# Linear attention and a multiplicative FFN on one core: q, k and v with 64 partitions of nine tokens per head, the heads split over the two partition halves, and the first batch in two head groups

## The chip, the core and the metric

The kernel runs on one core of one Trainium2 chip. The kernel's tiles in the on-chip memory (SBUF) have up to 128 partitions, their first axis; its matmuls leave their results in tiles in PSUM. The metric is device time in microseconds (us), lower is better. Each version was executed several times; the text gives the median and, in brackets, the lowest and highest.

## The reference, cut to what matters

Eight batches of eight heads, 576 tokens of 64 features each, go through linear attention; the result, 4608 tokens of 512 features, goes through two products, an elementwise product and two more products.

```python
def phi(x):  return np.where(x > 0, x, np.exp(x) - 1.0) + 1.0
# q, k, v: (8, 8, 576, 64) float32
kv  = einsum('bhsd,bhse->bhde', phi(k), v);  z = sum(phi(k), axis=2)
num = einsum('bhsd,bhde->bhse', phi(q), kv)
den = einsum('bhsd,bhd->bhs',  phi(q), z)[..., None] + 1e-06
x   = (num / den) transposed to (4608, 512)
a, b = x @ w1, x @ w2                      # 512 x 1024 each
out = (a * b @ w3) @ w_out                 # 1024 x 1024, 1024 x 512
```

phi is computed as max(x + 1, min(exp(x), 1)): one exp on ScalarE, one min and one add-max on VectorE. The kernel multiplies w3 by w_out once ("wf"), so that each token needs w1, w2 and wf only.

Of the kernel before, what the change touches and what calls it, by code (L numbers as in the profile page):

```python
# [8 lines left out]
F32 = mybir.dt.float32  # L9
# [9 lines left out]
def kernel(  # L19
# [18 lines left out]
    NJ = 4  # L38
    R = S - NJ * P
    JW = H * NJ * D  # L40
    RW = (H // 2) * D
    n_chunks = NTOK // NCH

# [3 lines left out]
    for b in range(0, B, 2):  # L47
        for key in [("J", b, j) for j in range(NJ)] + [("J", b + 1, j) for j in range(NJ)] + [("R", b, 0)]:
            tile_of[key] = len(order)
            order.append(key)  # L50
        tile_of["R", b + 1, 0] = tile_of["R", b, 0]
# [32 lines left out]
    vt = wpool.tile([P, NJ, H, D + 1], BF16)  # L84
    vr = wpool.tile([P, H // 2, D + 1], BF16)
    nc.gpsimd.memset(vt[:, :, :, D:D + 1], 1.0)
    nc.gpsimd.memset(vr[:, :, D:D + 1], 1.0)
# [4 lines left out]
    def load_qkv(name, src, b):  # L92
        t = ld.tile([P, JW + RW], F32, tag="ld", name=f"{name}32")
        ins = nc.sync.dma_start(
            out=t[:, 0:JW].rearrange("p (h x) -> p h x", h=H),
            in_=src[b, :, 0:NJ * P, :].rearrange("h (p j) d -> p h (j d)", j=NJ),
        )
        for hh in range(2):
            nc.sync.dma_start(
                out=t[hh * R:(hh + 1) * R, JW:].rearrange("p (h d) -> p h d", d=D),  # L100
                in_=src[b, hh * 4:(hh + 1) * 4, NJ * P:S, :].rearrange("h p d -> p h d"),
            )
        raw[name, b] = t
        return ins


    def phi_steps(name, b, dst_j, dst_r):
        x = raw[name, b]
        e = e_p.tile([P, JW + RW], BF16, tag="e", name="e")
        xv = x[:, 0:JW].rearrange("p (h j d) -> p h j d", h=H, j=NJ)  # L110
        ev = e[:, 0:JW].rearrange("p (h j d) -> p h j d", h=H, j=NJ)

        def ex(j0):
            nc.scalar.activation(  # L114
                out=ev[:, :, j0:j0 + 2, :], in_=xv[:, :, j0:j0 + 2, :], func=AF.Exp)
            nc.vector.tensor_scalar_min(  # L116
                out=ev[:, :, j0:j0 + 2, :], in0=ev[:, :, j0:j0 + 2, :], scalar1=1.0)

        def exr():
            nc.scalar.activation(out=e[:, JW:], in_=x[:, JW:], func=AF.Exp)  # L120
            nc.vector.tensor_scalar_min(out=e[:, JW:], in0=e[:, JW:], scalar1=1.0)

        def st(j):
            nc.vector.scalar_tensor_tensor(  # L124
                out=dst_j[:, j, :].rearrange("p (h d) -> p h d", h=H),
                in0=xv[:, :, j, :], scalar=1.0, in1=ev[:, :, j, :], op0=ALU.add, op1=ALU.max)

        def sr():
            nc.vector.scalar_tensor_tensor(
                out=dst_r, in0=x[:, JW:], scalar=1.0, in1=e[:, JW:],  # L130
                op0=ALU.add, op1=ALU.max)

        return dict(e0=lambda: ex(0), e2=lambda: ex(2), eR=exr, s0=lambda: st(0),
                    s1=lambda: st(1), s2=lambda: st(2), s3=lambda: st(3), sR=sr)

    ph = {}

    def k_steps(b):
        kj = phi_p.tile([P, NJ, DM], BF16, tag="kj", name="kj")
        kr = phi_p.tile([P, RW], BF16, tag="kr", name="kr")  # L140
        ph["k", b] = (kj, kr)
        return phi_steps("k", b, kj, kr)

    def q_steps(b):
        qj = phi_p.tile([P, NJ, DM], BF16, tag="qj", name="qj")
        qr = phi_p.tile([P, RW], BF16, tag="qr", name="qr")
        ph["q", b] = (qj, qr)
        return phi_steps("q", b, qj, qr)

    def v_unit(b, parts=(0, 2, 4)):  # L150
        x = raw["v", b]
        for j0 in parts:
            copy = nc.vector.tensor_copy if b == 0 and j0 else nc.scalar.copy
            if j0 < NJ:
                copy(out=vt[:, j0:j0 + 2, :, 0:D],  # L155
                     in_=x[:, 0:JW].rearrange("p (h j d) -> p j h d", h=H, j=NJ)[:, j0:j0 + 2])
            else:
                copy(out=vr[:, :, 0:D], in_=x[:, JW:].rearrange("p (h d) -> p h d", d=D))
# [3 lines left out]

    def kv_unit(b):

        kj, kr = ph["k", b]
        kvp = at_ps.tile([P, 2, 512], F32, tag="at", name="kvp")
        for hp in range(KC):
            o = kvp[:, hp // 2, (hp % 2) * 130:(hp % 2) * 130 + 130]
            for j in range(NJ):
                nc.tensor.matmul(  # L170
                    o, kj[:, j, hp * P:(hp + 1) * P],
                    vt[:, j, 2 * hp:2 * hp + 2, :].rearrange("p h e -> p (h e)"),
                    start=(j == 0), stop=False)
            hh, i = divmod(hp, 2)
            rows = slice(hh * R, (hh + 1) * R)
            nc.tensor.matmul(  # L176
                o, kr[rows, i * P:(i + 1) * P],
                vr[rows, 2 * i:2 * i + 2, :].rearrange("p h e -> p (h e)"),
                start=False, stop=True)
        t = att.tile([P, KC, 2, D + 1], BF16, tag="kv", name="kv")  # L180
        kvs[b] = t
        nc.vector.tensor_tensor(  # L182
            out=t.rearrange("p (a i) h e -> p a (i h e)", a=2), in0=kvp[:, :, 0:260],
            in1=mask.rearrange("p (a i) h e -> p a (i h e)", a=2), op=ALU.mult)
        return kvp


    def qt_load(b, part):
        qj, qr = ph["q", b]
        if part == 0:  # L190
            t = att.tile([P, NJ, KC, P], BF16, tag="qt", name="qt")
            src = qj.rearrange("p j c -> p (j c)")
            dst = t.rearrange("p j c t -> p (j c) t")
        else:
            t = att.tile([P, 2, P], BF16, tag="qtr", name="qtr")
            src, dst = qr, t
        qts[b, part] = t
        nc.sync.dma_start(out=dst, in_=src, transpose=True)

    def nat_unit(b, j):  # L200
# [4 lines left out]
        if j == 0:  # L205
            xns[b] = att.tile([P, NJ, H, D], BF16, tag="xn", name="xn")
        if j < NJ:
            n, dst = P, xns[b][:, j]
        else:
            n = R  # L210
            dst = xns[b, "R"] = att.tile([R, H, D], BF16, tag="xnr", name="xnr")
        for hp in range(KC):
            if j < NJ:
                w = qts[b, 0][:, j, hp, :]
            else:
                hh, i = divmod(hp, 2)
                w = qts[b, 1][:, i, hh * R:(hh + 1) * R]
            nc.tensor.matmul(nd[0:n, hp // 2, (hp % 2) * 130:(hp % 2) * 130 + 130], w,  # L218
                             t[:, hp].rearrange("p h e -> p (h e)"), start=True, stop=True)
        v4 = nd[0:n, :, 0:260].rearrange("p a (x e) -> p a x e", e=D + 1)  # L220
# [7 lines left out]
    def xt_load(b, part):  # L228
        if part == 0:
            i = tile_of["J", b, 0]  # L230
            dst = xt[:, i:i + NJ].rearrange("p j c t -> p (j c) t")
            src = xns[b].rearrange("p j h e -> p (j h e)")
        else:
            dst = xt[:, tile_of["R", b, 0], :, (b % 2) * R:(b % 2 + 1) * R]
            src = xns[b, "R"].rearrange("p h e -> p (h e)")
        nc.sync.dma_start(out=dst, in_=src, transpose=True)


    def first_tr():
        qj, _ = ph["q", 0]  # L240
        qt = qts[0, 0] = att.tile([P, NJ, KC, P], BF16, tag="qt", name="qt")
        tp = at_ps.tile([P, 2, 8, P], BF16, tag="at", name="tp")
        for j in range(NJ):
            for hp in range(KC):
                nc.tensor.transpose(  # L245
                    tp[:, j // 2, (j % 2) * KC + hp, :], qj[:, j, hp * P:(hp + 1) * P], ident)
            if j % 2:
                nc.vector.tensor_copy(
                    out=qt[:, j - 1:j + 1].rearrange("p j c t -> p (j c) t"), in_=tp[:, j // 2])

    def first_kv():
        kvp = kv_unit(0)
        t = kvz["z"] = att.tile([P, KC, 2, D], BF16, tag="kvz", name="kvz", bufs=1)
        n = kvz["n"] = att.tile([P, KC, 2, D], BF16, tag="kvn", name="kvn", bufs=1)
        m4 = mask.rearrange("p (a i) h e -> p a (i h) e", a=2)
        v4 = kvp[:, :, 0:260].rearrange("p a (x e) -> p a x e", e=D + 1)
        for dst, src in ((t, v4[:, :, :, D:D + 1].to_broadcast([P, 2, 4, D])),
                         (n, v4[:, :, :, 0:D])):
            nc.vector.tensor_tensor(
# [264 lines left out]
```

## The kernel before: the parts that the change touches

576 tokens are four times 128 and 64 left over. So each of q, k and v of a batch came as one large DMA over all 128 partitions (four tokens per partition and head, 1 KB rows) and two small ones for the rest, which put four heads on each partition half.

```python
NJ = 4; R = S - NJ * P          # R = 64 tokens left over
def load_qkv(name, src, b):
    t = ld.tile([P, JW + RW], F32, tag="ld", name=f"{name}32")
    ins = nc.sync.dma_start(                                   # 128 partitions, 1 KB rows
        out=t[:, 0:JW].rearrange("p (h x) -> p h x", h=H),
        in_=src[b, :, 0:NJ * P, :].rearrange("h (p j) d -> p h (j d)", j=NJ))
    for hh in range(2):                                        # the rest, 256 B rows
        nc.sync.dma_start(
            out=t[hh * R:(hh + 1) * R, JW:].rearrange("p (h d) -> p h d", d=D),
            in_=src[b, hh * 4:(hh + 1) * 4, NJ * P:S, :].rearrange("h p d -> p h d"))
```

A kv unit forms phi(k)ᵀ·[v, 1] of a batch, for each pair of heads four matmuls of 128 rows and one of 64. An nd unit multiplies transposed phi(q) with it (numerator and denominator), divides, and a transposing DMA brings the quotient to the layout xt that the FFN needs.

```python
def kv_unit(b):
    for hp in range(KC):                      # 4 pairs of heads
        for j in range(NJ):
            nc.tensor.matmul(o, kj[:, j, hp * P:(hp + 1) * P], vt[:, j, 2*hp:2*hp+2, :], ...)
        nc.tensor.matmul(o, kr[rows, ...], vr[rows, ...], start=False, stop=True)   # 64 rows
    # one multiplication by a mask, PSUM to SBUF
...
def o_unit(c, m):                             # 8 matmuls, then the output tile of 128 tokens
    if kind == "J": nc.gpsimd.dma_start(out=dst[:, j, :], in_=o_sb)
    else:           # two DMAs of 64 rows
```

The first batch goes step by step through whole tensors (phi of k, phi of q, 16 transposes, v, kv, nd), then FFN chunk 0 (512 tokens) follows. Loads of later batches are issued by the SP engine far ahead, into five buffers; weights and outputs are issued by GpSimd (POOL). From chunk 1 on a fixed schedule places the pieces of attention between FFN units ("F", 8 matmuls) and output units ("O").

## Time and profile before

| | before |
|---|---|
| time, first three runs | 285.53 us (283.41 to 285.62) |
| span of the profiled run, granted TensorE clock | 281.9 us, 0.975 |
| busy share of PE (TensorE), DVE (VectorE), ACT (ScalarE) | 86%, 55%, 47% |
| DMA: data moved, DMA queue of q, k, v (share of the 16 engines' span) | 51.63 MB, 55.3% |

The page of a profile cuts the span into 40 slices and gives busy tenths for each; "PEclk" is the clock that TensorE was granted, in tenths.

### The profile page before, as it was taken

How to read it: one execution, taken by the hardware profiler on the slowest of the kernel's cores; microseconds unless marked ns; L12 is line 12 of the kernel's file. 1: busy time of each engine (PE TensorE's matmuls, PEld its weight loads, DVE VectorE, ACT ScalarE, POOL GpSimd, SP SyncE). 2: the span in 40 equal slices, each digit the busy share in tenths (PEclk: the TensorE clock that was granted, in tenths of full speed). 3: DMA queues.
4: the chain of work that ended last, by engine and by line, in shares of the span. 5: the costliest groups of instructions: out<-in, count | busy, mean ns of one | idle time of the engine just before them, and what ended most of it. 6: DMA issues, size and time to landing. Idle time of an engine off the chain costs nothing.

```text
span 281.9 us, 3730 instructions
## 1 busy us (share of the span) xinstructions
PE 241.8 (86%) x1301; PEld 116.7 (41%) x1320; DVE 155.6 (55%) x326; ACT 132.7 (47%) x203; POOL 35.6 (13%) x70
## 2 busy tenths in 40 slices
PE   0045899999559977999999999999999999999990
PEld 0032245555225433545544444554544444444430
DVE  0863268418725995984895697499447221222300
ACT  2612467894804555455456555545532333333330
POOL 2380021000100000010110011011001001101021
PEclk9999999999959988999999999999999999999997
DMA  7999999999999979999999898906502501202122
GB/s 197 303 193 201 262 260 265 172 301 232 268 215 309 278 154 242 240 260 262 241 251 274 181 326 201 235 37 154 127 23 67 143 2 74 74 2 76 74 92 58
DMA packets 81139, 51.63 MB, mean 183 GB/s; under 512 B 48096, under 2 KB 77792, under 8 KB 81120
## 3 DMA queue, kind: packets, MB, share of 16 engines
q1 hardware_dynamic: 71744, 36.71, 55.3%
q0 software_dynamic: 9376, 14.68, 21.9%
q8 instruction: 10, 0.16, 0.2%
q14 instruction: 9, 0.07, 0.1%
HBM read 38.80 MB, written 9.44 MB: 171 GB/s over the span
## 4 chain that ended last, share of the span: by engine, by line
PE 76%; DMA 11%; DVE 6%; ACT 2%; issue 2%; SPq 1%; POOL 0%; POOLq 0%; DVEq 0%; ACTq 0%
PE a_ps L285 22%; PE b_ps L285 20%; PE o_ps L304 19%; DMA q<-in_q_dram 6%; PE wf_ps L356 4%; PE kvp L170 4%; DMA xt<-xn 3%; PE nd L218 3%; DMA qt<-qj 2%; PE kvp L176 2%; DVE qj L124 1%; PE w3p L350 1%; PE nd L269 1%; DVE xn L224 1%; ACT vt L155 1%
## 5 line engine op out<-in xcount | busy, mean ns | idle before, releaser
L285 PEld LDWEIGHTS <-w_sb 128*128 128x128 bf16 x576 | 55.8, 100 | 76.2 <-issue 10.1
L291 DVE TENSOR_TENSOR ab<-a_sb,b_ps 128x512 bf16<-128x512 f32 x72 | 49.2, 685 | 67.5 <-PE b_ps L285 57.4
L285 PE MATMUL a_ps<-xt,w_sb 128*128 128x512 bf16 x288 | 77.7, 390 | 8.8 <-DMA xt<-xn 6.1
L285 PE MATMUL b_ps<-xt,w_sb 128*128 128x512 bf16 x288 | 77.5, 389 | 0.0
L290 ACT COPY a_sb<-a_ps 128x512 f32<-128x512 f32 x72 | 41.7, 587 | 60.6 <-PE a_ps L285 59.3
L304 PE MATMUL o_ps<-wf_sb,ab 128*128 128x512 bf16 x272 | 66.2, 379 | 0.9 <-issue 0.2
L307 ACT COPY o_sb<-o_ps 128x512 f32<-128x512 f32 x36 | 21.1, 586 | 54.8 <-PE o_ps L304 52.8
L311 POOL DMA_DIRECT2D out_dram<-o_sb x32 | 17.4, 545 | 191.6 <-ACT o_sb L307 191.6
L304 PEld LDWEIGHTS <-ab 128*128 128x128 bf16 x288 | 27.6, 98 | 31.0
L124 DVE SCALAR_TENSOR_TENSOR qj<-q,e 128x512 bf16<-128x512 f32 x32 | 20.8, 684 | 0.4
L124 DVE SCALAR_TENSOR_TENSOR kj<-k,e 128x512 bf16<-128x512 f32 x32 | 20.6, 685 | 0.2
L224 DVE TENSOR_TENSOR xn<-nd,r 128x512 bf16<-128x512 f32 x28 | 19.4, 691 | 1.0
L116 DVE TENSOR_SCALAR e<-e 128x1024 bf16<-128x1024 bf16 x32 | 13.5, 422 | 10.5 <-ACT e L114 10.5
L114 ACT ACTIVATE e<-k 128x1024 bf16<-128x1024 f32 x16 | 16.9, 1060 | 4.7 <-DMA k<-in_k_dram 4.7
L114 ACT ACTIVATE e<-q 128x1024 bf16<-128x1024 f32 x16 | 16.4, 1058 | 2.1 <-DMA q<-in_q_dram 2.1
L170 PE MATMUL kvp<-vt,kj 128*128 128x130 bf16 x128 | 13.9, 233 | 3.3 <-ACT vt L155 1.7
L155 ACT CAST vt<-v 128x1024 bf16<-128x1024 f32 x15 | 15.0, 1045 | 1.7 <-DMA v<-in_v_dram 1.7
L245 PE MATMUL tp<-ident,qj 128*128 128x128 bf16 x16 | 2.2, 306 | 15.7 <-DVE qj L124 13.4
L356 PE MATMUL wf_ps<-wo_sb,w3t 128*128 128x512 bf16 x61 | 14.8, 379 | 0.3 <-issue 0.2
L182 DVE TENSOR_TENSOR kv<-kvp,mask 128x520 bf16<-128x520 f32 x8 | 5.6, 699 | 15.8 <-PE kvp L176 15.8
L218 PE MATMUL nd<-kv,qt 128*128 128x130 bf16 x112 | 11.0, 221 | 1.4 <-DMA qt<-qj 1.4
L218 PEld LDWEIGHTS <-qt 128*128 128x128 bf16 x112 | 8.6, 98 | 8.0 <-DMA qt<-qj 1.9
(49 smaller groups left out, 130.2 us busy)
## 6 DMA issues: line engine op xcount, KB each, us to landing
k<-in_k_dram SPq DMA_DIRECT2D x8, 1024.0 KB, 8.0
q<-in_q_dram SPq DMA_DIRECT2D x8, 1024.0 KB, 9.0
v<-in_v_dram SPq DMA_DIRECT2D x8, 1024.0 KB, 7.6
out_dram<-o_sb POOLq DMA_DIRECT2D x32, 256.0 KB, 4.1
w_sb<-in_moe_w_dram POOLq DMA_DIRECT2D x8, 256.0 KB, 7.1
w3b<-in_moe_w_dram POOLq DMA_DIRECT2D x8, 256.0 KB, 8.5
k<-in_k_dram SPq DMA_DIRECT2D x16, 64.0 KB, 7.1
q<-in_q_dram SPq DMA_DIRECT2D x16, 64.0 KB, 7.5
```

The source lines that it names most:

```text
L114: nc.scalar.activation(out=ev[:, :, j0:j0 + 2, :], in_=xv[:, :, j0:j0 + 2, :], func=AF.Exp)
L124: nc.vector.scalar_tensor_tensor(out=dst_j[:, j, :].rearrange("p (h d) -> p h d", h=H), in0=xv[:, :, j, :], scalar=1.0, in1=ev[:, :, j, :] ...
L155: copy(out=vt[:, j0:j0 + 2, :, 0:D], in_=x[:, 0:JW].rearrange("p (h j d) -> p j h d", h=H, j=NJ)[:, j0:j0 + 2])
L170: nc.tensor.matmul(o, kj[:, j, hp * P:(hp + 1) * P], vt[:, j, 2 * hp:2 * hp + 2, :].rearrange("p h e -> p (h e)"), start=(j == 0), stop=False)
L218: nc.tensor.matmul(nd[0:n, hp // 2, (hp % 2) * 130:(hp % 2) * 130 + 130], w, t[:, hp].rearrange("p h e -> p (h e)"), start=True, stop=True)
L224: nc.vector.tensor_tensor(out=dst.rearrange("p (a x) e -> p a x e", a=2), in0=v4[:, :, :, 0:D], in1=r[0:n].unsqueeze(3).to_broadcast([n, 2 ...
L285: nc.tensor.matmul(ps, w[:, kc, f * P:(f + 1) * P], xt[:, 4 * c:4 * c + 4, kc, :], start=(kc == 0), stop=(kc == KC - 1))
L290: nc.scalar.copy(out=a_sb, in_=a_ps)
L291: nc.vector.tensor_mul(out=abs_[c][:, f, :], in0=a_sb, in1=b_ps)
L304: nc.tensor.matmul(o_ps, ab[:, f, m * P:(m + 1) * P], wf_sb[:, f, :], start=(f == 0), stop=(f == FC - 1))
L307: nc.scalar.copy(out=o_sb, in_=o_ps)
L356: nc.tensor.matmul(ps, w3ts[i][:, kc, :], wo_sb[:, kc, :], start=(kc == 0), stop=(kc == FC - 1))
```

## The change

The intent: 576 is also 64 times 9. With nine tokens on each of 64 partitions per head, four heads on the lower and four on the upper partition half, nothing is left over. The loads become rows of 2304 B, the small rest loads and the rest pieces of phi vanish, and a kv unit becomes 36 half-height matmuls that alternate between the halves. The first batch is loaded and computed in two groups of heads, so that its work starts before all of it has landed. All of w3 is now loaded ahead of batch 1, and the schedule of the first chunks is rearranged.

```diff
-    NJ = 4
-    R = S - NJ * P
+    TP = S // 9
+    NJ = S // TP
@@ loads
-    def load_qkv(name, src, b):
-        t = ld.tile([P, JW + RW], F32, tag="ld", name=f"{name}32")
-        ins = nc.sync.dma_start(
-            out=t[:, 0:JW].rearrange("p (h x) -> p h x", h=H),
-            in_=src[b, :, 0:NJ * P, :].rearrange("h (p j) d -> p h (j d)", j=NJ),
-        )
+    def load_qkv(name, src, b, part=None):
+        if part is None or part == 0:
+            raw[name, b] = ld.tile([P, 4, X], F32, tag="ld", name=f"{name}32")
+        n, h0 = (4, 0) if part is None else (2, 2 * part)
+        for hh in range(2):
+            ins = nc.sync.dma_start(
+                out=raw[name, b][hh * TP:(hh + 1) * TP, h0:h0 + n, :],
+                in_=src[b, hh * 4 + h0:hh * 4 + h0 + n].rearrange("h (p j) d -> p h (j d)", j=NJ))
+        return ins
@@ kv: 36 half matmuls, the halves alternate and write different parts of kvp
+    def kv_mm(b, kvp, i):
+        for j in range(NJ):
+            for hh in range(2):
+                rows = slice(hh * TP, (hh + 1) * TP)
+                nc.tensor.matmul(
+                    kvp[:, hh, i * KVW:(i + 1) * KVW],
+                    ph["k", b][rows, i, j].rearrange("p u d -> p (u d)"),
+                    vt[rows, i, j].rearrange("p u e -> p (u e)"),
+                    start=(j == 0), stop=(j == NJ - 1))
@@ output: every tile is two DMAs of 64 rows
+        for i, (b, j) in enumerate(order[c * (NCH // P) + m]):
+            nc.gpsimd.dma_start(
+                out=out[b * S:(b + 1) * S, :].rearrange("(p j) n -> p j n", j=NJ)[:, j, :],
+                in_=o_sb[i * TP:(i + 1) * TP, :])
@@ first batch in two head groups
+    first_loads = [load(n, 0, i) for i in range(NI) for n in "kqv"]
+    ...
+    run(ks, "e0 s0 s1"); run(qs, "e0 s0 s1"); v_unit(0, (0,))      # (joined here)
+    run(ks, "e1 s2 s3"); run(qs, "e1 s2 s3"); first_tr(0)          # (joined here)
+    v_unit(0, (1,)); first_kv(0); first_tr(1)                      # (joined here)
+    fin = [first_nd(0, True), first_nd(2, True)]                   # own PSUM tiles
+    first_kv(1)
@@ order of loads
-    wl += [load_w3(0), load_w3(1)]
-    q1 = load_qkv("q", q, 1)
-    after(q1, wl[7])
+    wl += [load_w3(i) for i in range(FC)]
+    after(load("q", 1), wl[11])
... (other layout changes of phi, qt, nd, xt; new schedule strings for chunks 0 to 2)
```

## The prediction, made before the changed kernel ran

The forecast's sum is -7 (start) - 3.4 (kv) - 0 (middle) - 3 (chunks 1 and 2) + 0.3 (output), about -13, so 285.5 became 272.5 and then 272. The 3.4 us are six kv units of 0.57, from 1.4 us taken for a unit between 1.24 with full overlap of the half-height matmuls and 2.29 with none. That they would overlap was the main unknown of the forecast; no trace had shown it, and the 1.4 was the estimate. By "row groups" the prediction means the lower and the upper 64 partitions that a matmul's operands lie on. By "cold" it means stretches like 80 to 84 us and 104 to 108, where the granted clock was 0.54 and 0.57 and matmuls of 512 columns started some 0.42 us apart, where 0.216 is the step in the full part.

> **What bounds the kernel now.** I read the page first, for the engines and the slices of the span. Slices are 7 us each here.
>
> ```profile
> PE 241.8 (86%) x1301; PEld 116.7 (41%) x1320; DVE 155.6 (55%) x326; ACT 132.7 (47%) x203; POOL 35.6 (13%) x70
> PE   0045899999559977999999999999999999999990
> DMA  7999999999999979999999898906502501202122
> ```
>
> TensorE (PE) is the bound from slice 16 on. It is not the bound in the first 35 us, around slices 10 and 11, and around 14 and 15. The view by stretches puts numbers on that; its columns are the stretch, its length, busy time of PE, PEld, DVE, ACT and POOL, granted clock, DMA share, GB/s.
>
> ```profile
> 66.00:81.00 15.00, 8.76 (x52) 4.14 (x51) 11.12 (x27) 8.51 (x13) 2.19 (x4) 0.86 1.15 272
> 81.00:115.00 34.00, 30.15 (x165) 14.43 (x165) 23.97 (x52) 15.90 (x24) 0.54 (x1) 0.91 0.95 230
> 115.00:276.00 161.00, 158.54 (x830) 75.61 (x842) 89.28 (x189) 72.74 (x117) 18.65 (x35) 1.00 0.58 149
> ```
>
> So the kernel has three parts: a start, a middle with about 10 us of holes (15 - 8.76 plus 34 - 30.15), and 161 us with PE always at work. In the last part only less PE work helps. Third, the timeline of the start (start, duration, engine, instruction, [idle before]):
>
> ```profile
> 6.69 2.00 ACT L114 ACTIVATE e<-k 128x1024 bf16<-128x1024 f32 x2 [4.68 <-DMA k<-in_k_dram]
> 11.13 2.00 ACT L114 ACTIVATE e<-q 128x1024 bf16<-128x1024 f32 x2 [2.13 <-DMA q<-in_q_dram]
> 15.16 1.05 ACT L155 CAST vt<-v 128x1024 bf16<-128x1024 f32 x1 [1.72 <-DMA v<-in_v_dram]
> 22.64 0.70 DVE L182 TENSOR_TENSOR kv<-kvp,mask 128x520 bf16<-128x520 f32 x1 [2.86 <-PE kvp L176]
> 27.42 0.58 PE L285 MATMUL a_ps<-xt,w_sb 128*128 128x512 bf16 x1 [1.37 <-DVE xt L274]
> 35.86 1.02 PE L285 MATMUL a_ps<-xt,w_sb 128*128 128x512 bf16 x4
> ```
>
> k, q and v of batch 0 land whole, at 6.7, 11.1 and 15.2; then everything is serial, the first FFN matmul runs at 27.4, and the FFN runs without gaps only from 35.86. Fourth, the timeline of PE in the full part, for the small matmuls:
>
> ```profile
> 129.43 0.39 PE L170 MATMUL kvp<-vt,kj 128*128 128x130 bf16 x4
> 129.76 0.23 PE L176 MATMUL kvp<-vr,kr 64*128 64x130 bf16 x1
> 129.92 0.40 PE L170 MATMUL kvp<-vt,kj 128*128 128x130 bf16 x4
> ...
> 131.40 1.04 PE L285 MATMUL a_ps<-xt,w_sb 128*128 128x512 bf16 x4
> ...
> 136.59 0.40 PE L218 MATMUL nd<-kv,qt 128*128 128x130 bf16 x4
> 136.82 1.02 PE L285 MATMUL a_ps<-xt,w_sb 128*128 128x512 bf16 x4
> ```
>
> Starts, not durations, are what counts, as matmuls overlap. Four nd matmuls take 136.82 - 136.59 = 0.23 us, 58 ns each. A kvp group of four full and one 64-row matmul takes 129.92 - 129.43 = 0.49, though five at 58 ns are 0.29: each change between 128 and 64 rows costs 0.10. A whole kv unit is four such groups, 131.40 - 129.43 = 1.97 us, of which 8 changes are 0.8. Last, the middle:
>
> ```profile
> 71.30 4.12 SPq L236 DMA_TRANSPOSE xt<-xn  x1
> 80.58 1.89 PE L285 MATMUL a_ps<-xt,w_sb 128*128 128x512 bf16 x4 [6.09 <-DMA xt<-xn]
> ```
>
> Chunk 1 waits 6.1 us for a transposing DMA that took 9.2 us from issue beside a full DMA system, and its first 8 matmuls come at half speed.
>
> [...] matmuls of 512 columns start 0.43 us apart after the wait at 80.58 and 0.216 in the full part. [...] those loads have rows of 256 B and 1 KB, and still moved about 300 GB/s at 3 to 11 us.
>
> **The change, part by part.**
>
> *Start, two head groups.* Half of k is 0.59 MB. At 302 GB/s (3 to 7 us of the trace), with first bytes at about 2.5, the six half loads land at about 4.6, 6.4, 8.4, 10.3, 12.5 and 15. Durations for 1152 and 576 columns follow from the rows for 1024, 512 and 256: exp 1.17 us, min 0.455, add-max 0.75. DVE then does k0 (min, two add-max) to 8.0, q0 to 10.0, k1 (after its exp at 11.5) to 13.4, q1 (exp 12.5 to 13.7) to 15.7. PE transposes group 0 at 10.0 and does its kv matmuls to 13.4, all inside the wait for the second half. Group 0's masks come at 15.7 to 16.5 (DVE in order), group 1's transposes at 15.7 to 17, nd of pairs 0 and 2 until 18.7, kv of group 1 until 20 to 20.6, its masks to 21.3, nd of pairs 1 and 3 to 22.6. ACT has 12 steps by then (4 exp, 2 v copies, 6 transpose copies of 0.3 to 0.6) and Ln and exp of the first two pairs done at 21.1, of the last at 24.5. xt of the last pair is ready at 25.1. The first 16 FFN matmuls, half at the cold 0.43, end at 27.5 to 29.5, against 35.86. Gain: 6.5 to 8; I take **7**.
>
> *Layout, kv.* Before, 16 full and 4 half matmuls per batch; now 36 half ones with the two halves alternating[...]. Cost if the row groups overlap: 18 x 0.058 + 2 x 0.10 = 1.24 us, so 0.73 saved. If they do not: 36 x 0.058 + 0.2 = 2.29, so 0.32 lost. [...] I take 1.4, that is 0.57 saved. Six such units (batches 2 to 7) lie where PE is the bound: **3.4**; batch 1's is another 0.6 in the middle. nd stays 20 matmuls with one narrow group.
>
> *Layout, elementwise.* The separate rest pieces vanish. DVE per tensor was 2 x 0.422 + 0.225 + 4 x 0.684 + 0.425 = 4.23, now 2 x 0.455 + 4 x 0.75 = 3.91; 0.64 per batch for k and q. ACT saves about 0.57 per batch. In the full part DVE is 89 of 161 us, so this is worth **nothing** there by itself, only somewhat in the middle.
>
> *Middle.* Batch 1's phi moves from beside chunk 0's FFN to beside the w3 product, and its kv and nd now follow that product, spread over the output units. PE work is the same. ACT has there 6 x 1.03 + 8 x 0.60 + 4 x 1.17 + 2 x 1.17 = 18 us against PE's 6 x 0.45 + 8 x 1.73 = 16.5, so ACT may cost 1 us. After kv the DVE needs 0.7 + 4 x 1.1 + 0.45 + 0.75 = 6.3 us (with waits 7.5) before the transposing DMA may go, and PE has 3.9 us left to cover it: the stall stays, some 4 to 6 us. But the loads of batch 3 now queue behind that DMA, so it should take nearer its median of 5.2 than 9.2. Net: **0** (0.6 and perhaps 2 for the DMA, against ACT and the later kv).
>
> *Chunks 1 and 2.* At 101 to 112 the kernel before lost 1.1, 0.7 and 1.4 us to v and qt, and several us of cold clock. The new order puts three FFN units, then two output units, ahead of kv, and loads are rows of 2304 B. One stall on the new xt at the start of chunk 2 should remain. Gain about **3** of the 7 at stake (4 idle, 3 cold).
>
> *Output.* All 36 tiles are two DMAs of 64 rows now, 72 issues of 0.54 us on POOL instead of 40: 39 us over 200, hidden; the last one ends perhaps **0.3** later.
>
> Sum: -7 - 3.4 - 0 - 3 + 0.3 = -13; 285.5 - 13 = 272.5. The trace's own run was 283.65 us, so the middle of the three times is a little high; I go to **272**.
>
> **Rivals.** *Row groups do not overlap.* For it: the trace never shows two 64-row matmuls at once. [...] It would cost 6 x (0.57 + 0.32) = 5.3 us: about 277. *The saved start comes back as a wait.* All of w3 now streams before batch 1's loads, and by 40 us the kernel has asked for some 14 MB; the DMA row shows 9 in most of the first 14 slices. If the weights or k1 are late, PE that starts 7 us earlier waits 7 us later: 277 to 279. Against: before, 10.5 MB (read side) had come by about 28 us, so the weights for F2 to F7 should be there. *ACT bounds the middle.* With 18 us of 16.5, plus FFN copies left over: 2 us at most, 274. *Everything fits*: overlap full, stalls of the middle gone: 285.5 - 8 - 5 - 6 = 266.
>
> **Range and chances.** The centre 272 with the four ways round it gives 265 to 279 for 8 in 10. 2% of 285.53 is 5.7, so same begins at 279.8. That needs two of the rivals at once. Chances: faster 0.91, same 0.08, slower 0.01.
>
> **What would show it.** In the timeline of the start: the first kv group before 14 us, FFN without gaps from about 28. In the timeline of PE in the full part: a kv unit of 1.2 to 1.6 us from the first kvp start to the next a_ps start, and chunks repeating every 23.3 to 23.7 us instead of 24.08. In the waits: one wait for xt of 4 to 6 us near 70, and no wait for qt or vt. It is wrong if a kv unit takes over 2 us, if w3 or k loads appear as waits of PE before 60 us, or if the first FFN stretch begins later than 31.

## More of the kernel before

The chain that ended last is the path of work followed back from the last instruction.

```profile
q1 hardware_dynamic: 71744, 36.71, 55.3%
...
PE 76%; DMA 11%; DVE 6%; ACT 2%; issue 2%; SPq 1%; POOL 0%; POOLq 0%; DVEq 0%; ACTq 0%
```

The first line is packets, MB and share of the 16 engines' span. The second says that 76% of the chain is TensorE's own work and 11% is waiting for DMAs. So TensorE bounds the kernel, but the DMA system isn't idle beside it.

## The result, and the profile after

Ratios here and below are the mean time of one kernel's fast runs over that of the other's fast runs of the same rounds, so they aren't quite the ratio of the quoted medians. The bracket after a ratio is its 95% interval.

| | before | after |
|---|---|---|
| time, median (range), 4 runs each | 285.31 us (283.41 to 285.62) | 312.44 us (312.29 to 315.08) |
| ratio | 1 | 1.0988 [1.0912, 1.1064] |
| span, granted clock of the profiled run | 281.9 us, 0.975 | 310.5 us, 0.932 |

The changed kernel is 10% slower, where 5% faster was predicted. The result is correct.

On the page of the kernel after, TensorE's work has hardly changed (242.8 us busy, against 241.8), but its row of slices (7.8 us each, counted from 0) now has holes up to slice 16 and again at 19 and 26, and the DMA row has nines down to slice 26:

```profile
PE   0248999595197439399789999959999999999960
...
DMA  7999999999989999999999999990781713303250
...
q1 hardware_dynamic: 46592, 36.64, 60.5%
...
PE 57%; DMA 31%; DVE 3%; SPq 2%; ACT 2%; issue 2%; POOL 1%; POOLq 0%; ACTq 0%; DVEq 0%
```

The chain gives 31% to DMAs, where it was 11%. The queue of the loads moves the same bytes (36.64 MB) in fewer packets (46592 for 71744), and yet its packets took 60.5% of 310.5 us, 187.9 us of each engine, where it was 55.3% of 281.9, 155.9 us. These are 32 us more DMA time for the same data.

The view by stretches shows the same in one line. Its columns are stretch, length, busy time and count of PE, PEld, DVE, ACT, POOL, granted clock, DMA share, GB/s. First the kernel before, then after:

```profile
80.00:130.00 50.00, 45.51 (x245) 21.65 (x248) 35.94 (x80) 24.80 (x38) 2.16 (x4) 0.93 1.02 242
130.00:215.00 85.00, 84.63 (x481) 41.90 (x489) 60.87 (x135) 43.92 (x69) 8.68 (x16) 1.00 0.74 184
```

```profile
80.00:130.00 50.00, 30.30 (x195) 14.12 (x196) 24.27 (x46) 19.29 (x24) 2.09 (x4) 0.83 1.03 197
130.00:215.00 85.00, 76.96 (x457) 36.53 (x464) 57.92 (x117) 39.19 (x53) 11.50 (x22) 0.92 1.01 205
```

From 80 to 130 us the DMA share is full in both (1.02 and 1.03), but it yields 242 GB/s before and 197 after. PE loses 15 us of work in this stretch and 8 in the next.

PE's timeline names the waits (in brackets: idle before, and what ended it):

```profile
61.92 0.70 PE L141 MATMUL kvp<-vt,kphi 64*128 64x130 bf16 x18 [2.61 <-ACT vt L127]
...
84.48 1.89 PE L267 MATMUL a_ps<-xt,w_sb 128*128 128x512 bf16 x4 [8.66 <-DMA xt<-xn]
...
130.13 0.29 PE L179 MATMUL nd<-kv,qt 128*128 128x130 bf16 x2 [3.54 <-DMA qt<-qphi]
```

The waits for xt and qt are waits for transposing DMAs, which stand in the same queue as the loads. In the chain, such a DMA took some 10 us from issue to landing, and v of batch 1 took 18:

```profile
42.44 18.18 DMA v<-in_v_dram
...
74.57 9.86 DMA xt<-xn
...
121.62 10.05 DMA qt<-qphi
```

Last the start, in ACT's timeline of the kernel after. Every half load (0.59 MB) is one exp or copy, which runs as soon as it has landed:

```profile
6.10 1.16 ACT L113 ACTIVATE e<-k 128x1152 bf16<-128x1152 f32 x1 [4.07 <-DMA k<-in_k_dram]
8.55 1.16 ACT L113 ACTIVATE e<-q 128x1152 bf16<-128x1152 f32 x1 [1.29 <-DMA q<-in_q_dram]
11.11 1.17 ACT L127 CAST vt<-v 128x1152 bf16<-128x1152 f32 x1 [1.40 <-DMA v<-in_v_dram]
13.70 1.16 ACT L113 ACTIVATE e<-k 128x1152 bf16<-128x1152 f32 x1 [1.42 <-DMA k<-in_k_dram]
16.27 1.16 ACT L113 ACTIVATE e<-q 128x1152 bf16<-128x1152 f32 x1 [1.41 <-DMA q<-in_q_dram]
18.83 1.17 ACT L127 CAST vt<-v 128x1152 bf16<-128x1152 f32 x1 [0.27 <-DMA v<-in_v_dram]
```

One half load comes every 2.55 us, which is 0.59 MB / 2.55 us = 231 GB/s. Before, whole tensors of 1.18 MB came 4.0 to 4.4 us apart, 266 to 293 GB/s. So the loads are slower from the start, before the middle's traffic.

The trace records each DMA packet with its size and duration. Counted for the loads' queue (a count of our own over those records, not a view of the profile):

```
          packet size x count   median  mean    sum / 16 engines
before     1024 B x 24576        46 ns   58 ns    88.8 us
before      256 B x 45056        18 ns   23 ns    65.7 us
after      2304 B x 12288       181 ns  171 ns   131.5 us
after       256 B x 32512        18 ns   27 ns    55.2 us
```

Here is the loss: a packet of 2304 B should take 2304/1024 x 46 = 104 ns if packets cost by the byte; it takes 181, 12.7 GB/s per engine instead of 22.3. The large loads cost 131.5 us of each engine instead of 88.8. They carry 28.3 MB and not 25.2, as the rest loads have gone into them: before, 12288 of the 256 B packets were rest loads, and all the other packets of that size are the transposing DMAs'. By the byte the growth would be to 99.9 us, so some 32 us are lost.

Three reasons were open. **Half the partitions:** a load now covers partitions 0 to 63 or 64 to 127 alone. **Long rows:** packets of 2304 B may cost more per byte than those of 1024 B. **Order:** w3 ahead of batch 1 and the new schedule put more traffic at the wrong time, and packets are slow because they queue. The first was not looked at by the prediction. The trace fits it: 12.7 GB/s for a packet is a little over half of 22.3. The experiments had to show whether it is this.

### The profile page after: what moved, and what is told of

It reads as the page before. It is cut to its first block, busy times and chain, and to the rows that moved or that the text cites. A ratio compares the mean times of both kernels' runs of the same rounds, so it can differ in the third digit from the quotient of the medians.

```text
span 310.5 us, 3924 instructions
## 1 busy us (share of the span) xinstructions
PE 242.8 (78%) x1430; PEld 116.0 (37%) x1450; DVE 151.6 (49%) x291; ACT 134.6 (43%) x187; POOL 52.4 (17%) x103
## 3 DMA queue, kind: packets, MB, share of 16 engines
q1 hardware_dynamic: 46592, 36.64, 60.5%
## 4 chain that ended last, share of the span: by engine, by line
PE 57%; DMA 31%; DVE 3%; SPq 2%; ACT 2%; issue 2%; POOL 1%; POOLq 0%; ACTq 0%; DVEq 0%
PE o_ps L286 18%; PE a_ps L267 18%; PE b_ps L267 17%; DMA qt<-qphi 9%; DMA xt<-xn 7%; DMA v<-in_v_dram 6%; DMA w3b<-in_moe_w_dram 4%; DMA w_sb<-in_moe_w_dram 3%; DMA k<-in_k_dram 3%; PE nd L179 3%; PE kvp L141 2%; SPq L98 1%; ACT vt L127 1%; DVE xn L186 1%; POOL w_sb L304 1%
## 5 line engine op out<-in xcount | busy, mean ns | idle before, releaser
L291 POOL DMA_DIRECT2D out_dram<-o_sb x72 | 37.7, 528 | 225.8 <-ACT o_sb L289 225.8
L114 DVE TENSOR_SCALAR e<-e 128x1152 bf16<-128x1152 bf16 x32 | 14.9, 467 | 29.7 <-ACT e L113 29.4
L179 PE MATMUL nd<-kv,qt 128*128 128x130 bf16 (+1 forms) x144 | 15.5, 230 | 14.6 <-DMA qt<-qphi 11.1
L117 DVE SCALAR_TENSOR_TENSOR qphi<-q,e 128x576 bf16<-128x576 f32 x32 | 23.2, 754 | 0.5
L117 DVE SCALAR_TENSOR_TENSOR kphi<-k,e 128x576 bf16<-128x576 f32 x32 | 23.0, 754 | 0.4
L113 ACT ACTIVATE e<-k 128x1152 bf16<-128x1152 f32 x16 | 18.6, 1166 | 8.1 <-DMA k<-in_k_dram 8.1
L127 ACT CAST vt<-v 128x1152 bf16<-128x1152 f32 x16 | 18.0, 1168 | 8.1 <-DMA v<-in_v_dram 8.1
L179 PEld LDWEIGHTS <-qt 128*128 128x128 bf16 (+1 forms) x144 | 10.9, 105 | 26.4 <-DMA qt<-qphi 13.1
L113 ACT ACTIVATE e<-q 128x1152 bf16<-128x1152 f32 x16 | 18.5, 1165 | 2.7 <-DMA q<-in_q_dram 2.7
L209 PE MATMUL tp<-ident,qphi 128*128 128x128 bf16 x18 | 2.3, 310 | 17.4 <-DVE qphi L117 17.4
L141 PE MATMUL kvp<-vt,kphi 64*128 64x130 bf16 x288 | 10.9, 224 | 3.3 <-ACT vt L127 3.3
```

Source lines behind the costliest of these rows:

```text
L113: nc.scalar.activation(out=e[:, hs], in_=x[:, hs], func=AF.Exp)
L117: nc.vector.scalar_tensor_tensor(out=dst[:, h // 2, :, h % 2, :], in0=x[:, h].rearrange("p (j d) -> p j d", d=D), scalar=1.0, in1=e[:, h]. ...
L127: (copy or nc.scalar.copy)(out=vt[:, i, :, :, 0:D].rearrange("p j u d -> p u j d"), in_=raw["v", b][:, 2 * i:2 * i + 2].rearrange("p u (j ...
L141: nc.tensor.matmul(kvp[:, hh, i * KVW:(i + 1) * KVW], ph["k", b][rows, i, j].rearrange("p u d -> p (u d)"), vt[rows, i, j].rearrange("p u ...
L179: nc.tensor.matmul(nd[0:n, hp // 2, (hp % 2) * KVW:(hp % 2 + 1) * KVW], qts[b][:, hp, m * P:m * P + n], t[:, hp].rearrange("p h e -> p (h ...
L291: nc.gpsimd.dma_start(out=out[b * S:(b + 1) * S, :].rearrange("(p j) n -> p j n", j=NJ)[:, j, :], in_=o_sb[i * TP:(i + 1) * TP, :])
```

## The experiments

All runs below have correct results, unless it is said otherwise. The kernels in a group shared a chip and the runs of the kernel before.

### First group: partitions, rows or order (before: 284.66 us, 282.92 to 286.17)

**b_half** puts only the suspected cause into the kernel before: its large load in two contiguous halves of 64 partitions, with the same 1 KB rows, bytes and schedule.

```diff
-        ins = nc.sync.dma_start(
-            out=t[:, 0:JW].rearrange("p (h x) -> p h x", h=H),
-            in_=src[b, :, 0:NJ * P, :].rearrange("h (p j) d -> p h (j d)", j=NJ),
-        )
+        for hh in range(2):
+            ins = nc.sync.dma_start(
+                out=t[hh * 64:(hh + 1) * 64, 0:JW].rearrange("p (h x) -> p h x", h=H),
+                in_=src[b, :, hh * 256:(hh + 1) * 256, :].rearrange("h (p j) d -> p h (j d)", j=NJ))
```

> The kernel before, with each large q/k/v load issued as two loads of 64 partitions each; rows stay 1 KB, nothing else changes. Theory HALF (a load that writes only one half of the partitions runs its packets at about half rate[...]): the 1 KB packets go from a median of 46 ns to about 90, and the kernel becomes DMA bound and slower, 300 us or more against 285. Theory SIZE (packets of 2304 B are slow in themselves): packets stay at 46 ns median, time within 2% of before. Theory ORDER (the new order of loads is to blame): as SIZE.

Measured: 320.9 us (319.4 to 321.81), ratio 1.1265 [1.12, 1.133]. The 1 KB packets took 86 ns (median) instead of 46, and its queue is even busier than that of the kernel after (64.9% for 60.5), with nines down to slice 26 in the DMA row of its page as well:

```profile
q1 hardware_dynamic: 72128, 36.71, 64.9%
```

The halves alone, without any other part of the change, cost more than the whole change did.

**a_128** undoes the halves in the kernel after, from batch 1 on, and keeps rows of 2304 B, order and schedule: even heads go to the lower partition half and odd heads to the upper, so one DMA covers all 128 partitions. The order of heads is put right where nd is written to SBUF.

```diff
+        if part is None:
+            return nc.sync.dma_start(
+                out=raw[name, b],
+                in_=src[b].rearrange("(a u) (p j) d -> (u p) a (j d)", u=2, j=NJ))
@@ nat_unit
-            out=dst.rearrange("p (a x) e -> p a x e", a=2), in0=v4[:, :, :, 0:D],
+            out=dst.rearrange("p (a x) e -> p a x e" if b == 0 else "p (x a) e -> p a x e", a=2),
+            in0=v4[:, :, :, 0:D],
```

> The changed kernel, with each load from batch 1 on issued as one load of all 128 partitions with the same 2304 B rows: even heads on one partition half and odd heads on the other, undone where the normalised output is written. Result stays right. HALF: 2304 B packets fall from a median of 181 ns to about 92-100, time near 270 us (262 to 276), faster than before. SIZE: packets stay near 180 ns, time stays within 2% of 312. ORDER: as SIZE.

Measured: 280.23 us (279.78 to 281.22), ratio 0.9847 [0.9793, 0.99] (faster, but the interval reaches below and above a gain of 2%), 32.2 us below the kernel after. The same 2304 B packets now took 93 ns (24.8 GB/s per engine), and the loads 89.2 us of each engine. So the rows aren't the reason. The queue and the two stretches of its profile:

```profile
q1 hardware_dynamic: 46256, 36.64, 50.8%
```

```profile
80.00:130.00 50.00, 43.72 (x311) 21.46 (x310) 37.18 (x75) 25.33 (x33) 4.19 (x8) 0.97 0.96 271
130.00:215.00 85.00, 84.03 (x534) 40.84 (x532) 61.45 (x126) 42.42 (x60) 15.71 (x30) 1.00 0.74 182
```

The bytes per second at a full DMA share are back (271 GB/s for 197), and so is PE's work (43.72 and 84.03 us for 30.30 and 76.96).

**a_split** keeps the halves and cuts each row of the kernel after into packets of 1024 and 1280 B.

```diff
-            ins = nc.sync.dma_start(
-                out=raw[name, b][hh * TP:(hh + 1) * TP, h0:h0 + n, :],
+            for lo, hi in ((0, 256), (256, X)):
+                ins = nc.sync.dma_start(
+                    out=raw[name, b][hh * TP:(hh + 1) * TP, h0:h0 + n, lo:hi],
```

> The changed kernel, loads still by partition halves, but each row of 2304 B moved as two packets of 1024 and 1280 B by two loads. SIZE: 1024 B packets at 46-60 ns as in the kernel before, total load time falls by a third, time below 290. HALF: 1024 B packets near 85 ns, 1280 B near 100, time within 2-3% of 312, perhaps a little worse for twice the issues.

Measured: 317.78 us (316.8 to 318.32), ratio 1.1157 [1.1097, 1.1217]. Packets of 1024 B took 79 ns and of 1280 B 106, again 12 to 13 GB/s per engine. Shorter rows don't help on half the partitions.

**a_order** lets batch 1's loads start after w1 and w2, ahead of w_out and w3.

```diff
-    after(load("q", 1), wl[11])
+    after(load("q", 1), wl[7])
```

> The changed kernel, with the load of q of batch 1 released by the last w1/w2 load, as in the kernel before, and not by the second w3 load. ORDER: the waits between 50 and 130 us shrink and the time falls by 10 us or more. HALF and SIZE: packets as slow as before, time within 2% of 312, since the same bytes still take the same DMA time.

Measured: 312.49 us (308.33 to 313.59, all four runs), ratio 1.0892 [1.078, 1.1004]. Its profiled run was slow, and so was one more of the four; the two fast ones, on which the ratio rests, took 311.91 and 308.33 us. ORDER forecast 10 us or more, so the order isn't the reason for the loss; a gain of a few us by it is not excluded.

### Second group: which partitions, or how many; the rest of the difference (before: 283.74 us, 281.9 to 285.72)

**b_evenodd** is the closest control for b_half: again two DMAs of 64 partitions each with 1 KB rows, but every second partition instead of a contiguous half. In the expectations PORTS is the name of the theory that it matters which partitions a load covers, COUNT of the theory that it matters how many.

```diff
+        for u in range(2):
+            ins = nc.sync.dma_start(
+                out=t[u:P:2, 0:JW].rearrange("p (h x) -> p h x", h=H),
+                in_=src[b, :, 0:NJ * P, :].rearrange("h (r u j) d -> u r h (j d)", u=2, j=NJ)[u])
```

> The kernel before, each large load issued as two loads of 64 partitions again, but every second partition (even, then odd) instead of a contiguous half; rows stay 1 KB. PORTS[...]: 1 KB packets stay at a median of 46 to 60 ns and the time is within 3% of before. COUNT (any load of 64 partitions is slow, or any load cut in two): packets near 86 ns as in the run with contiguous halves, time near 320 us.

Measured: 283.76 us (282.51 to 285.02), ratio 0.9978 [0.9836, 1.012]; packets 46 ns, and the queue is no busier than before:

```profile
q1 hardware_dynamic: 72128, 36.71, 52.7%
```

Two DMAs, half the partitions in each, and nothing is lost (283.76 us against 283.74). What counts is which partitions, not how many.

**b_quarter** is b_half with four DMAs of 32 contiguous partitions.

```diff
+        for u in range(4):
+            ins = nc.sync.dma_start(
+                out=t[u * 32:(u + 1) * 32, 0:JW].rearrange("p (h x) -> p h x", h=H),
+                in_=src[b, :, u * P:(u + 1) * P, :].rearrange("h (p j) d -> p h (j d)", j=NJ))
```

> The kernel before, each large load issued as four loads of 32 contiguous partitions; rows stay 1 KB. PORTS: [...] packets stay near the 86 ns of the run with halves, not slower; time 318 to 330 us (more issues). COUNT: packets slow further, to 150 ns or more, time above 360 us.

Measured: 316.94 us (316.47 to 317.42), ratio 1.1144 [1.103, 1.1259]; packets 85 ns. Thirty-two partitions are as fast per packet as sixty-four (85 ns and 86). A rate in proportion to the count of partitions is excluded. (This and b_evenodd have two runs each.) What stays untested: each of these edits also changes the order in which DRAM is read, which no run changed alone, and no run tried other choices of partitions than contiguous ones and every second one. That every large load over a contiguous half or quarter was slow (b_half, b_quarter, a_split, the kernel after) and every one spread over all 128 or every second partition was fast (before, b_evenodd, a_128) speaks for the partitions. By what mechanism was not shown.

One thing was overlooked: the outputs of the kernel after are DMAs of 64 contiguous partitions too. Their packets (4096 B x 2304 in the queue of GpSimd, by the same count) took a median of 169 ns before, 269 in the kernel after and 274 in a_128, which left them as they are. So a_128 has the halves out of its later loads, not out of its outputs; what that costs was not tried.

**a_out** takes up the end of the kernel. In the trace GpSimd ends with a drain: 8.04 us after 90 DMAs issued in the kernel after, 5.45 us after 58 in the kernel before, which is some 81 ns for each DMA more ((8.04 - 5.45) / 32, an estimate). From the last landing to the end of the span it is 6.2 us after (310.5 - 304.3) and 3.6 before (281.9 - 278.3). a_out is a_128 with the output DMAs of chunks 6 to 8 issued by SP, whose loads are done by then.

```diff
-            nc.gpsimd.dma_start(
+            (nc.gpsimd if c < 6 else nc.sync).dma_start(
```

> The changed kernel with 128-partition loads, and with the output DMAs of the last three chunks issued by SP instead of GpSimd. Theory DRAIN (the 8.0 us drain of GpSimd that ends the kernel grows with the DMAs it has issued, 90 against 58 before with 5.4 us): the drain shrinks to about 6 us or hides wholly beside the last chunks, the span ends within 4 us after the last output lands, time 274 to 277 instead of 280. Rival: the end is set by the landing of the last outputs, then the time stays within 1 us of 280.

Measured: 274.39 us (273.12 to 275.72), ratio 0.9645 [0.9548, 0.9743], 5.8 us below a_128's median of the other group (by the ratios, 0.9847 - 0.9645, it is 2% of the kernel before, the same). The drain is 6.08 us for 66 DMAs and lies at 216 us beside other work; the span ends 1.05 us after the last landing. This is the best correct version and beats both kernels.

**a_cover** tried to remove what was left of the stalls at the start of chunks 1 and 2 in a_128 (3.87 us for xt at 74.58, 2.74 us at 97.36, for which the timeline names no releaser): batch 1's loads earlier, and two output units ahead of chunk 2's first FFN unit, to cover its wait.

```diff
-    after(load("q", 1), wl[11])
+    after(load("q", 1), wl[7])
@@
-    SECOND = """F0 Qs2 Qs3 T O0 V Lk O1 KV Ke0 F1 ...
+    SECOND = """Qs2 Qs3 T O0 V Lk O1 F0 KV Ke0 F1 ...
```

> The changed kernel with 128-partition loads, q of batch 1 released by the last w1/w2 load, and the first two output units of chunk 1 put ahead of the first FFN unit of chunk 2. Theory STALLS (what is missing to the forecast is waits left in the middle: 3.9 us for xt before chunk 1, 2.7 us before chunk 2): 2 to 5 us less than the run with 128-partition loads alone, 275 to 278. Rival: DVE or ACT sets the pace there, then the time stays within 1 us of 280.

Measured: 279.22 us (279.03 to 281.16), ratio 0.9834 [0.976, 0.9907], no better than a_128: a miss. Its PE timeline shows why:

```profile
75.34 1.89 PE L272 MATMUL a_ps<-xt,w_sb 128*128 128x512 bf16 x4 [3.78 <-DMA xt<-xn]
...
99.29 3.48 PE L291 MATMUL o_ps<-wf_sb,ab 128*128 128x512 bf16 x9 [2.04 <-DVE ab L278]
```

The first wait stayed, and the second became a wait for VectorE, which was busy 9.69 of the 10 us from 90 to 100. Here covering a wait for a DMA was of no use, as the covering work waited for a full engine. What would remove these last 6 us is open.

### Third group: the end, the start and the new matmuls (before: 284.23 us, 283.92 to 284.96)

**b_out** measures the end alone: the kernel before with its last three chunks' outputs issued by SP (the edit of a_out).

```diff
-            nc.gpsimd.dma_start(out=dst[:, j, :], in_=o_sb)
+            (nc.gpsimd if c < 6 else nc.sync).dma_start(out=dst[:, j, :], in_=o_sb)
```

> The kernel before, with only the output DMAs of the last three chunks moved from GpSimd to SP. DRAIN: the 5.4 us drain at the end is then hidden too; the span should end about 1.5 us after the last landing instead of 3.6, so 2 to 3 us less than before, 281 to 283. Rival: within 1 us of before.

Measured: three runs of 280.78, 281.04 and 281.91 us, ratio 0.9891 [0.9866, 0.9916], and one of 855.23 us, the profiled one, which is counted as slow and isn't explained here. By the ratio the tail is worth 3.1 us in the kernel before, whose drain is shorter (below the 2% that count as faster, but clear of the noise), and 5.8 us in a_128.

**a_first** is a_out with batch 0's six half loads over 128 partitions as well. Its result is wrong: the heads of batch 0 aren't put back in order. The work is the same.

```diff
+        return nc.sync.dma_start(
+            out=raw[name, b][:, h0:h0 + n],
+            in_=src[b].rearrange("(a u) (p j) d -> (u p) a (j d)", u=2, j=NJ)[:, h0:h0 + n])
```

> The changed kernel with 128-partition loads and the last outputs by SP, and with the first batch's six half loads also issued as loads of 128 partitions. Its result is wrong on purpose for batch 0 (the heads come in another order). PORTS: the half loads of batch 0 land at about 5, 7, 9, 11, 13 and 15 instead of 6.1, 8.6, 11.1, 13.7, 16.3 and 18.8, the FFN runs without gaps 2 to 3.5 us earlier than at 29, time 271 to 273 instead of 274.4. Rival: the start is bound by the serial work after landing, or the gain is given back at a later wait: time within 1 us of 274.4.

Measured: 269.85 us (269.36 to 271.53), ratio 0.9501 [0.9467, 0.9535]. ACT's start, where a whole half load is again one instruction:

```profile
4.53 1.16 ACT L120 ACTIVATE e<-k 128x1152 bf16<-128x1152 f32 x1 [2.51 <-DMA k<-in_k_dram]
6.00 1.16 ACT L120 ACTIVATE e<-q 128x1152 bf16<-128x1152 f32 x1 [0.31 <-DMA q<-in_q_dram]
7.95 1.17 ACT L134 CAST vt<-v 128x1152 bf16<-128x1152 f32 x1 [0.78 <-DMA v<-in_v_dram]
```

q comes 1.5 us after k and v 1.95 us after q, 0.59 / 1.5 = some 390 and 0.59 / 1.95 = some 300 GB/s, where it was 231. The FFN runs without gaps from 24.52 instead of 29.34 (a_out), and 4.5 us of these 4.8 remain at the end.

**a_nogroup** takes the two head groups out of a_out: batch 0 in the old order k, q, v, with phi of all, then transposes and kv.

```diff
-    first_loads = [load(n, 0, i) for i in range(NI) for n in "kqv"]
+    first_loads = [load(n, 0, i) for n in "kqv" for i in range(NI)]
@@
-    run(ks, "e0 s0 s1")
-    run(qs, "e0 s0 s1")
-    v_unit(0, (0,))
-    run(ks, "e1 s2 s3")
-    run(qs, "e1 s2 s3")
+    run(ks, "e0 s0 s1 e1 s2 s3")
+    run(qs, "e0 s0 s1 e1 s2 s3")
     first_tr(0)
+    v_unit(0, (0,))
```

> The changed kernel with 128-partition loads and the last outputs by SP, but batch 0 in the old order: all of k, then all of q, then all of v, and the transposes and kv only after all of phi. Theory GROUPS (the two head groups are what brings the FFN forward): the FFN runs without gaps from 33 to 36 us instead of 29, time 4 to 6 us longer, 278 to 280. Rival: the overlapped kv matmuls and ACT copies alone bring it forward: time within 2 us of 274.4.

Measured: 274.69 us (273.1 to 275.25), ratio 0.9642 [0.9605, 0.968], as a_out. The first FFN matmul group without gaps, in PE's timeline of a_nogroup, then of a_out:

```profile
28.32 1.02 PE L272 MATMUL a_ps<-xt,w_sb 128*128 128x512 bf16 x4
```

```profile
29.34 1.02 PE L272 MATMUL a_ps<-xt,w_sb 128*128 128x512 bf16 x4
```

Without the groups the FFN starts even a microsecond sooner, and the time is the same. The theory that the head groups bring the earlier start of a_out has fallen. v lands in both at about 18.8, and from v on everything waits for the same kv. The control was made only with half loads that come late, though; with the loads of a_first the groups may be worth something, and that is left open. What is shorter than before is the way after kv: from the end of its matmuls, where DVE's first masked product starts (22.64), to the FFN without gaps (35.86) it was 13.2 us in the kernel before; from the start of the second group's kv matmuls in a_out (22.29) it is 7.1. There nd has PSUM tiles of its own, the reciprocals have two buffers, and ACT copies the transposes; besides, TensorE goes at twice the pace there: matmuls of 512 columns that don't wait start some 0.215 us apart from 24.64 on, where before they started 0.43 apart until 32.07. Which of these counts most wasn't tried.

**a_serial** is a_out with a kv unit's matmuls in the order of all of the lower half, then all of the upper, instead of in turn.

```diff
-        for j in range(NJ):
-            for hh in range(2):
+        for hh in range(2):
+            for j in range(NJ):
```

> The changed kernel with 128-partition loads and the last outputs by SP, with the 36 half-height kv matmuls of a batch in another order: all of the lower partition half, then all of the upper[...]. If it is the alternation that makes them overlap, a kv unit takes 36 x 58 ns + 0.2 = 2.3 us instead of 1.25 and the time grows by about 6 us, to 280. If not, the unit stays at 1.2 to 1.3 us and the time at 274.4 within 1 us.

Measured: 277.71 us (276.64 to 278.58), ratio 0.9765 [0.9736, 0.9794], 3.3 us above a_out's; 6 were expected. PE's timeline of a_serial, then of a_128, whose kv unit is the one of the change:

```profile
125.88 1.62 PE L145 MATMUL kvp<-vt,kphi 64*128 64x130 bf16 x36
127.43 1.04 PE L272 MATMUL a_ps<-xt,w_sb 128*128 128x512 bf16 x4
```

```profile
148.43 1.03 PE L272 MATMUL b_ps<-xt,w_sb 128*128 128x512 bf16 x4
149.39 1.23 PE L145 MATMUL kvp<-vt,kphi 64*128 64x130 bf16 x36
150.55 1.04 PE L272 MATMUL a_ps<-xt,w_sb 128*128 128x512 bf16 x4
...
172.77 1.22 PE L145 MATMUL kvp<-vt,kphi 64*128 64x130 bf16 x36
```

In a_serial the 36 matmuls take 127.43 - 125.88 = 1.55 us; in turn they take 150.55 - 149.39 = 1.16. So the alternation is worth 0.39 us per unit. The records of single matmuls (read one by one from the trace, not a view of the profile) show why it is no more. In a_128 the matmuls start in pairs, one for each half, 3 to 4 ns apart, and the pairs follow every 59 ns, as one matmul of 128 rows does: 18 pairs, full overlap. In a_serial neighbours of the same half start 55 to 66 ns apart too, so a half-height matmul is not quicker. But each run of nine overlaps the next run, which is of the other half, by four matmuls: 126.179 and 126.238 of the lower half, 126.187 and 126.253 of the upper. Three such overlaps of four save 12 of 36 steps. So the order of a_serial did not turn the overlap off, as it was meant to, and the expected 2.3 us, which counts no overlap, was not tested.

## Why the prediction was wrong, point by point

**The step that failed** is the one on which the other gains stand: "Half of k is 0.59 MB. At 302 GB/s (3 to 7 us of the trace), with first bytes at about 2.5, the six half loads land at about 4.6, 6.4, 8.4, 10.3, 12.5 and 15", and, for the middle, "loads are rows of 2304 B" as a gain. It carried over the rate of loads that cover 128 partitions to loads that cover 64. The half loads were used at 6.10, 8.55, 11.11, 13.70, 16.27 and 18.83. The working judged the loads by the size of their rows alone; the destination's partitions, which the diff shows plainly, were not looked at. b_half shows that this one property is enough for the loss, a_128 that without it the loss is gone (312.4 to 280.2), and b_evenodd and b_quarter that it is the choice of partitions and not their number.

**What the runs showed in its place.** A half load came every 2.55 us, 231 GB/s instead of 302. The start hid that (see below), the middle didn't. The first FFN without gaps began 6.8 us earlier than before (35.86 to 29.07), but chunk 1's began 3.9 us later (80.58 to 84.48), batch 4's kv 17.4 us later (129.43 to 146.86), and batch 7's 26.9 us later (201.68 to 228.53). So the terms "Middle: 0" and "Chunks 1 and 2: about 3" are where the time went.

**The warning stood in the prediction's own lines.** The stretches of 66 to 115 us have a DMA share of 1.15 and 0.95, and the DMA row has nines well past the middle. The prediction priced the loads' landings at the start only, and took the transfers of the middle as given. A passage of it also took the 48096 packets that the page counts under 512 B for rows of loads: only 12288 of them are, the others belong to the transposing DMAs (32768 of 256 B) or have 4 B.

**The rivals.** None was this one. "The saved start comes back as a wait" had the right form. But the reason it gave, w3 ahead of batch 1, isn't the main one by a_order, and it was sized at 5 to 7 us where the loss was 32 against a_128. Its sign, waits of PE for w3 or k before 60 us, showed only as 0.62 us for w3 at 38.48; the long waits came later and were for xt and qt.

**The start.** 29.07 lies in the predicted 27.5 to 29.5, by two errors that cancel. The last v came at 18.83 instead of 15, and the way from there to the FFN took 10.2 us instead of 12.5 to 14.5 (half of the first 16 FFN matmuls were taken at 0.43 us, but 13 of their 15 steps were 0.21 to 0.25). So that this number came out right was luck. And the head groups, to which the prediction gave the gain, bring nothing as long as the half loads are late (a_nogroup). With loads over all partitions the start would be better than predicted, 24.52 (a_first).

**kv.** Right, and a little better than assumed: 1.26 us per unit in a_128 (from 148.43 + 0.86, when the matmuls ahead of it are through, to 150.55), against the 1.4 taken, 1.24 for full overlap and 1.97 before. From kv to kv the three later chunks take 24.59, 23.38 (172.77 - 149.39) and 23.66 us, against 24.08 before and the predicted 23.3 to 23.7; the first of them still waits for qt, which the prediction excluded. The theory beneath it, that the gain comes from the overlap of matmuls on the two partition halves, is shown: pairs start 3 to 4 ns apart.

**Elementwise.** Right in size: exp 1.166 us, min 0.467, add-max 0.754 in the rows of the page (1.17, 0.455, 0.75). That it has no effect on the full part fits too: the chunk of 23.38 us is 0.70 shorter than before, and the kv unit alone is 0.71 shorter.

**Middle and chunks 1 and 2.** Too favourable even without the fault in the loads. In a_128 chunk 1's FFN starts 6.0 us earlier than before (80.58 to 74.58), so the predicted zero for the middle holds. But batch 4's kv, two chunks later, starts only 4.6 us earlier (129.43 to 124.81). The predicted gain of 3 was a loss of 1.4, although two shorter kv units lie in the stretch, with stalls of 3.87 and 2.74 us that remain.

**Output.** The larger number of DMAs was seen, their cost was not: +0.3 was predicted, and the end grew by 2.6 us (6.2 for 3.6) with GpSimd's drain, which none of the views of busy time lists.

The path of the time, then: 312.4 after, 280.2 with loads over all partitions from batch 1 on, 274.4 with the last outputs by SP, 269.9 with batch 0's loads over all partitions too (not a correct kernel). Without the halves in its later loads the change is worth 1.5%, and with the drain out of the way some 3.5%. But b_out takes the drain out of the way of the kernel before too, for 1.1%; against it the change is worth some 2.5% (0.9645 / 0.9891 = 0.975), half of what was predicted.

## What to carry to other kernels

Before a load's layout is changed, write down which partitions each single DMA covers, not only its row size and bytes: loads into contiguous halves ran at about half the packet rate here (86 ns for 1 KB instead of 46), and renaming which heads go to which half let one DMA cover all partitions at no cost that shows. If the DMA row of the profile is full, price a change of the transfers for the whole kernel, and the median time of a packet by size, before and after, finds such a loss at once. Look at what stands between the last landing and the end of the span, too: moving the last outputs to another issuing engine gave 3.1 to 5.8 us.
